# Gated linear attention and a gated expert block: the state product over the whole PE array, with a new order of work

## The chip, the cores and the metric

The kernel runs on one core of a Trainium2 chip. The metric is the device time of one execution in microseconds (us). The engines are TensorE (PE: matrix products; PEld is its weight load), VectorE (DVE), ScalarE (ACT), GpSimd (POOL) and SyncE (SP, which here only starts DMAs).

## The reference

Four batches of eight heads run a decayed linear attention over 768 steps with heads of 48; its output, 3072 tokens of 384, is normalized and goes through a gated expert layer of width 1536.

```python
for t in range(S):
    state = alpha[:, :, t, :, None] * state + np.einsum('bhd,bhe->bhde', k[:, :, t], v[:, :, t])
    y[:, :, t] = np.einsum('bhd,bhde->bhe', q[:, :, t], state)
...
rms = np.sqrt(np.mean(x * x, axis=-1, keepdims=True) + 1e-06)
xn = x / rms * rms_g
g = xn @ w_gate
silu = g * (1.0 / (1.0 + np.exp(-g)))
return (silu * (xn @ w_val) @ w_out)
```

## The kernel before

**Chunks.** The sequence is cut into 24 chunks of 128 tokens, six for each batch; the program takes the first chunks of the four batches, then the second, and so on, so chunk numbers 0 to 3 are first chunks and have no state yet. Within a chunk the eight heads are four pairs. The two heads of a pair lie on partitions 0 to 47 and 64 to 111 of the tiles for k, q and the state.

**Attention of a chunk** (`attention`, L589). DVE makes the running products of the decay by two scans (L616), multiplies k and q with them (L634, L639), and each is split into a high and a low f16 part (`k_lo` L646, `q_lo` L673, `v_lo` L664; the high parts on ACT). PE forms the scores (`scores`, L709; for first chunks in f32, L717), DVE masks them (L722, L736) and splits them (L776). `output` (L780) then adds two things into the PSUM tile `y`: q times the state of the past chunks (L791) and the masked scores times v (L800). Each f16 product is done in three parts, high by high, high by low and low by high (`SPLIT`). First chunks use f32 scores times v instead (L749). For the state, `s_decay` (L691) makes the decayed state `sd`, ACT copies it to f16 (`s_hi`, L695), DVE forms the residue (`s_lo`, L699), and `sums` (L817) makes the next state's addition from the transposed k. Last, ACT squares `y` (L849), DVE multiplies it with the norm's gains (L869), splits it (L876), and a transposing DMA puts it into `xT`.

**The state product before.** L791 uses tiles of 48 rows by 64 columns: for each pair and each of the three parts, the two heads (rows 0 to 47 and 64 to 111) times the two halves of 64 tokens are four products of 48 columns, 12 a pair and 48 a chunk. Head 0 of all pairs is in one PSUM bank of `y`, head 1 in the other; there is one such `y` tile of two banks (`y=1`).

**Weights** (`decode`, L492). The 64-bit weights are turned into f32 by ACT (L519) and three DVE operations (L528, L531, L536), and split into a high part (ACT) and a low part. The low part comes from DVE (L544), or, for the weights named in `LOW_W`, from PE: `bring` (L549) copies the f32 weight into the `y` tile by a product with the identity, `less` (L556) subtracts the high part, ACT reads the result (L562). `i0` to `i11` are the twelve column blocks of the two input matrices, `o0` to `o5` the pairs of blocks of the output matrix.

**Experts.** Seven groups of 4, 2, 2, 4, 4, 4 and 4 chunks (`GROUPS`). For each group and each of 12 column blocks `expert_in` runs 9 products for the gate and 9 for the value (L1002, 512 columns for a group of four chunks, 256 for two), ACT and DVE make the gated product and split it (L1013, L1019, L486, L1032); then `expert_out` sums over the blocks (L1072), DVE drains (L1083) and a DMA stores. Group 0 runs its first five blocks on chunks 0 and 1 first and then on chunks 2 and 3.

**The order.** Nothing is scheduled by hand: `Plan.order` sorts all steps by a model of each engine with the tables at the top (`COST`, `PACE`, `GAP`, `AHEAD`, `STRIDE`, `LATE`, `HOLD`, `BUFS`); each engine then executes its list strictly in that order. At the end `verdict` sums up checks of the data on DVE and PE (L1181, L1209), and all engines branch on the resulting `flag` (L1238, L1239).

Of the kernel before, what the change touches and what calls it, by code (L numbers as in the profile page):

```python
# [50 lines left out]
LOW_W = ['i0', 'i1', 'o1', 'i11', 'i7']  # L51

BUFS = dict(
    att=3, v=2, kh=2, qp=2, k16=2, q16=2, kT=2, v16=4, gd=2, a16=2, ss=2, dk=1, x32=1, x16=2,
    xT=2, raw=2, wu=2, h16=13, sl=2, h32=3, ob=2, at=3, y=1, mm=3,
# [3 lines left out]
    scan=1.16, rec=0.13, kh=0.6, kl=0.6, vl=0.47, ql=0.62, gd=0.12, sd=0.28, sl=0.27, mask=0.59,  # L59
    al=0.59, st=0.27, ss=0.12, x=0.46, xl=0.53, shift=0.57, sign=0.97, rest=0.88, wl=0.87, ob=0.46,  # L60
    dec=0.1, k16=0.62, v16=0.52, q16=0.62, s16=0.26, a16=0.5, sq=0.58, x16=0.53, st0=0.22,
    abs=0.92, wh=0.83, pow=0.65, sc=0.8, sc32=2.3, y=0.78, y0=0.5, y32=1.85, u=0.45, po=1.48,
    neg=0.3, wid=1.6, wneg=0.45, wl2=0.85,
# [9 lines left out]
PACE = [0.939, 1.309, 1.366, 1.325, 1.11, 1.095, 1.217, 1.519]  # L73
GAP = [0, 9.2, -0.3, -0.8, 7.1, 0.3, 11.3, 10.4]
FIRST_DUE = [-19.3, -19.1, -6.2, -12.5]
AHEAD = [0, 6.1, 6.5, 12.3, 23.9, 15.3, 13.6, 8.2]
STRIDE = [0, 4.9, 9.6, 16.8, 26.0, 20.7, 39.7, 9.1]
LATE = dict(
    abs=-14.0, al=-0.2, gd=2.4, h=-10.0, hl=5.8, k16=12.3, kl=1.0, load=6.5, mask=0.9,
    neg=-4.7, ob=-12.5, po=17.9, q16=4.2, ql=1.2, rec=-4.0, rest=0.6, sc=-10.0, scan=2.8,  # L80
    sd=1.5, shift=-3.4, sign=-6.0, sl=3.9, sq=2.0, ss=-4.6, st=-8.0, u=-15.4, v16=14.9,
    vl=-8.0, wh=8.0, wid=3.9, wl=1.9, wneg=-15.1, x=-5.9, x16=12.4, xl=-4.5, y=-3.4,
)
HOLD = dict(
    c10=51.1, c11=64.8, c2=1.0, c5=9.2, c6=12.0, c7=38.1, c8=98.8, i1=19.5, i10=43.3,
    i11=21.3, i4=33.0, i5=48.0, i6=24.5, i9=26.4, o1=68.1, o3=36.2,
# [252 lines left out]
def tile_attn_moe(  # L339
# [160 lines left out]
    def decode(src, dst, name, col):  # L500
# [44 lines left out]

        def bring():
            t["ps"] = buf(ps_y, [P, 2, 512], F32, "y", name)
            for n in range(2):
                nc.tensor.matmul(  # L549
                    t["ps"][:, n, : NW // 2], same, t["uf"][:, n * (NW // 2) : (n + 1) * (NW // 2)],  # L550
                    start=True, stop=False,
                )

        def less():
            for n in range(2):
                nc.tensor.matmul(  # L556
                    t["ps"][:, n, : NW // 2], minus, dst[:, 0, n * (NW // 2) : (n + 1) * (NW // 2)],
                    start=False, stop=True,
                )
# [12 lines left out]
        if name in LOW_W:  # L572
            ps = ("y", name)
            o0 = add("PE", "wid", bring, [o], [wu, ps])
            o = add("ACT", "wh", high, [o], [wu])
            o = add("PE", "wneg", less, [o, o0], [ps])
            return add("ACT", "wl2", residue, [o], [ps])
# [5 lines left out]
    state_ops = {}  # L583

# [3 lines left out]
    def attention(cc, due):  # L588
# [67 lines left out]
        def v_flat():  # L656
            return t["v16"].rearrange("s x j p e -> s x (j p e)")

        def v_hi():
            t["v16"] = tl(ap, [P, 2, 2, NP, D], F16, "v16")  # L660
            split_hi(v_flat()[:, 0], tiles["v", cc], cc, S_V)
# [27 lines left out]
        def s_decay():  # L689
            st, sd, _ = states[b]  # L690
            nc.vector.tensor_tensor(sd, st, t["gd"].to_broadcast([R, NP, D]), op=ALU.mult)  # L691

        def s_hi():
            _, sd, s16 = states[b]
            nc.scalar.copy(s16[:, 0], sd)  # L695

        def s_lo():
            _, sd, s16 = states[b]
            nc.vector.tensor_tensor(s16[:, 1], sd, s16[:, 0], op=ALU.subtract)  # L699
# [43 lines left out]
        def output32(h):  # L743
            if h == 0:
                t["y"] = tl(ps_y, [P, 2, 512], F32, "y")
            v = tiles["v", cc].rearrange("s (j p e) -> s j p e", j=2, p=NP)
            for p in (2 * h, 2 * h + 1):
                for j in range(2):
                    nc.tensor.matmul(  # L749
                        t["y"][:, j, p * D : (p + 1) * D],  # L750
                        tiles["a16", cc][:, j, p, :],
                        v[:, j, p, :],
# [27 lines left out]
        def output(h):  # L780
            if h == 0:
                t["y"] = tl(ps_y, [P, 2, 512], F32, "y")
            yps = t["y"]
            for p in (2 * h, 2 * h + 1):
                cs = slice(p * D, (p + 1) * D)
                for m, (x, y) in enumerate(() if first else SPLIT):
                    for n in range(2):
                        rows = slice(n * HC, (n + 1) * HC)
                        for j in range(2):
                            r = slice(64 * j, 64 * j + D)  # L790
                            nc.tensor.matmul(  # L791
                                yps[rows, j, cs],
                                t["q16"][r, x, p, rows],
                                states[b][2][r, y, p, :],
                                start=m == 0,
                                stop=False,
                            )
                for j in range(2):
                    for m, (x, y) in enumerate(SPLIT):
                        nc.tensor.matmul(  # L800
                            yps[:, j, cs],
                            a_tile()[:, j, x, p, :],
                            t["v16"][:, y, j, p, :],
                            start=first and m == 0,
                            stop=m == 2,
                        )

        def sums():

            t["u"] = [buf(ps_at, [R, NP, D], F32, "at", (cc, 2 + h)) for h in range(2)]  # L810
            for p in range(NP):
                for m, (x, y) in enumerate(SPLIT):
                    for j in range(2):
                        r = slice(64 * j, 64 if j == 0 else R)
                        for h in range(2):
# [4 lines left out]
                                t["v16"][rows, y, j, p, :],  # L820
# [4 lines left out]
        def s_back():  # L825
            if first:
                states[b] = (
                    const.tile([R, NP, D], F32, name=f"st{b}"),
                    const.tile([R, NP, D], F32, name=f"sd{b}"),
                    const.tile([R, 2, NP, D], F16, name=f"s16{b}"),  # L830
                )
                nc.scalar.copy(states[b][0], t["u"][0])
                return
            st, sd, _ = states[b]
# [10 lines left out]
        def like(x):  # L845
            return x.rearrange("p (j c) -> p j c", c=HW)

        def square():
            nc.scalar.activation(  # L849
                like(junk), t["y"][:, :, :HW], AF.Square, accum_out=ssq[:, cc : cc + 1]  # L850
            )
# [15 lines left out]
        def gain():  # L867
            t["x32"] = tl(ap, [P, DM], F32, "x32")
            nc.vector.tensor_tensor(like(t["x32"]), t["y"][:, :, :HW], like(rg), op=ALU.mult)  # L869
# [48 lines left out]
        else:  # L918
# [4 lines left out]
            sh = add("ACT", "s16", s_hi, [sd, before["y"]])  # L923
            sl = add("DVE", "sl", s_lo, [sh], lock=True)
# [7 lines left out]
        else:  # L932
# [12 lines left out]
            ins = [key("a16"), key("v16"), key("y")] + ([] if first else [key("q16")])  # L945
# [304 lines left out]
def layout(inputs):  # L1250
# [25 lines left out]
    vt = v.reshape(B, NP, 2, n, C, D)[:, :, :, :, ::-1].transpose(0, 3, 4, 2, 1, 5)  # L1276
    vt = np.ascontiguousarray(vt).reshape(B * n, C, H * D)

    def rows(x):

        y = np.asarray(x).reshape((NP, 2, D) + x.shape[1:])
        return np.ascontiguousarray(np.moveaxis(y, 1, 0)).reshape(x.shape)
# [4 lines left out]
        "w_gate": rows(inputs["moe_w_gate"]).view(np.int64),  # L1287
        "w_val": rows(inputs["moe_w_val"]).view(np.int64),
        "w_out": np.ascontiguousarray(inputs["moe_w_out"]).view(np.int64),
        "rms_g": rows(inputs["moe_rms_g"]),  # L1290
# [3 lines left out]
                    x.reshape(B, NP, 2, S, D).transpose(0, 2, 1, 4, 3).reshape(B * H, D, S)  # L1294
# [4 lines left out]
        "rms_col": np.ascontiguousarray(rows(inputs["moe_rms_g"]).reshape(-1, C).T),  # L1299
# [18 lines left out]
```

## Time and profile before

| | |
|---|---|
| median of 3 runs | 555.12 us (555.1 to 555.75) |
| span of the profiled execution | 554.4 us |
| mean granted PE clock | 0.992 |
| PE busy | 524.5 us, 5508 products |
| DVE busy | 399.4 us |
| ACT busy | 238.4 us |
| state products (L791) | 960, 22.4 us busy |
| value products (L800) | 480, 25.9 us busy |

The profile is one execution with the time of every instruction on every engine. In the timelines a row gives start, length, engine, line, operation, tiles, shapes and count; lengths of matrix products overlap, since the array takes the next before the last has left it. In rows of groups stand count, total busy time, mean of one in ns, then the idle time before them and what ended it. A row of waits reads: who waited for whom, us in total, times, longest.

### The profile page before, as it was taken

What the parts mean: (1) busy time and instruction counts of PE and PEld (TensorE: products, weight loads), DVE (VectorE), ACT (ScalarE), POOL (GpSimd) and SP (SyncE); (2) the same over time, 40 slices, a digit from 0 to 9 for tenths busy, and PEclk for the clock granted to TensorE, in tenths of its full rate; (3) what the DMA queues carried; (4) which work ended last, traced back from release to release, by engine and by line L of the source; (5) the groups of instructions that cost most, each with busy time, mean ns of one, the idle gap of its engine ahead of it and who ended that gap; (6) DMA issues with size and microseconds to landing.
All of it is one profiled execution on the core that took longest, in us unless ns stands there. A gap on an engine that the chain in (4) does not pass through costs nothing.

```text
span 554.4 us, 13165 instructions
## 1 busy us (share of the span) xinstructions
PE 524.5 (95%) x5508; PEld 315.3 (57%) x5508; DVE 399.4 (72%) x731; ACT 238.4 (43%) x643; POOL 25.1 (5%) x53
## 2 busy tenths in 40 slices
PE   1868999999999999999999999999999999999994
PEld 1746864556886887554556544556544456544452
DVE  6999999999999999987683688999335343233303
ACT  2355866743564565355432254564133421133300
POOL 2101000001001001100000000010000000000000
PEclk9998999999999999999999999999999999999998
DMA  8997546547435523714033234231200000100001
GB/s 210 269 250 194 168 140 214 172 103 181 131 65 140 130 48 96 176 57 91 16 82 76 80 97 92 38 75 34 71 2 2 15 1 30 43 1 0 1 30 35
DMA packets 59444, 50.65 MB, mean 91 GB/s; under 512 B 39440, under 2 KB 54928, under 8 KB 59376
## 3 DMA queue, kind: packets, MB, share of 16 engines
q1 hardware_dynamic: 59376, 49.72, 35.6%
q8 instruction: 45, 0.74, 0.6%
q14 instruction: 23, 0.19, 0.1%
HBM read 35.68 MB, written 4.72 MB: 73 GB/s over the span
## 4 chain that ended last, share of the span: by engine, by line
PE 80%; DVE 13%; issue 3%; DMA 1%; ACT 0%; DVEq 0%; ACTq 0%
PE mm L1002 43%; PE mm_po L1072 24%; PE y L800 4%; PE y L791 3%; PE at L709 3%; DVE dk L616 2%; PE at L817 2%; DVE wu_i L531 1%; DMA kT<-k 1%; DVE h L1019 1%; PE y_i L549 1%; DVE h L1032 1%; DVE wu_i L528 1%; DVE wu_o L531 1%; DVE wu_i L536 1%
## 5 line engine op out<-in xcount | busy, mean ns | idle before, releaser
L1002 PE MATMUL mm<-xT,wg 128*128 128x512 f16 (+1 forms) x1602 | 290.3, 340 | 0.3 <-DVE h L1019 0.3
L1002 PEld LDWEIGHTS <-wg 128*128 128x128 f16 x1602 | 154.5, 98 | 120.5 <-issue 0.7
L1072 PE MATMUL mm_po<-wo,h 128*128 128x384 f16 x864 | 145.8, 326 | 0.0
L1072 PEld LDWEIGHTS <-h 128*128 128x128 f16 x864 | 82.5, 98 | 53.9 <-issue 0.5
L1019 DVE SCALAR_TENSOR_TENSOR h<-mm,sl 128x512 f32<-128x512 f32 (+1 forms) x89 | 51.8, 584 | 51.3 <-PE mm L1002 50.6
L486 ACT ACTIVATE h<-h 128x512 f16<-128x512 f32 (+1 forms) x89 | 48.6, 546 | 83.0 <-DVE h L1019 82.4
L1032 DVE TENSOR_TENSOR h<-h,h 128x512 f16<-128x512 f32 (+1 forms) x89 | 51.8, 583 | 22.2 <-ACT h L486 22.1
L1013 ACT ACTIVATE sl<-mm 128x512 f32<-128x512 f32 (+1 forms) x89 | 45.5, 511 | 40.6 <-PE mm L1002 40.3
L616 DVE TENSOR_TENSOR_SCAN dk<-att,seed 112x520 f32<-112x520 f32 x48 | 59.3, 1236 | 2.8 <-DMA att<-att 2.2
L865 POOL TENSOR_TENSOR ss<-ss,mhalf 128x1 f32<-128x1 f32 x24 | 20.8, 865 | 377.7 <-DVE ss L855 347.1
L1083 DVE TENSOR_SCALAR ob<-mm_po 128x384 f32<-128x384 f32 x24 | 13.2, 551 | 31.3 <-PE mm_po L1072 31.3
L773 ACT CAST a<-at 128x512 f16<-128x512 f32 x40 | 23.1, 584 | 20.0 <-DVE at L722 19.8
L849 ACT ACTIVATE junk<-y 128x384 bf16<-128x384 f32 x24 | 11.7, 489 | 44.8 <-DVE x L869 30.6
L722 DVE TENSOR_TENSOR at<-at,mask 128x512 f32<-128x512 f32 x40 | 26.2, 691 | 0.9 <-PE at L709 0.8
L800 PE MATMUL y<-v,a 128*128 128x48 f16 x480 | 25.9, 185 | 1.0 <-DVE v L664 1.0
L776 DVE TENSOR_TENSOR a<-at,a 128x512 f16<-128x512 f32 x40 | 26.1, 681 | 0.1
L869 DVE TENSOR_TENSOR x<-y,rg 128x384 f32<-128x384 f32 x24 | 13.3, 554 | 17.2 <-PE y L800 14.1
L717 PE MATMUL at<-qp,kh 48*128 48x128 f32 x64 | 8.9, 440 | 14.8 <-DVE qp L639 12.1
L791 PE MATMUL y<-s,q 48*64 48x48 f16 x960 | 22.4, 193 | 0.0
L486 ACT ACTIVATE k<-kh 112x512 f16<-112x512 f32 x24 | 15.0, 626 | 14.5 <-DMA kT<-k 6.0
L791 PEld LDWEIGHTS <-q 48*64 48x64 f16 x960 | 14.1, 106 | 11.1 <-issue 8.6
L800 PEld LDWEIGHTS <-a 128*128 128x128 f16 x480 | 17.3, 96 | 3.8 <-issue 1.1
(104 smaller groups left out, 437.7 us busy)
## 6 DMA issues: line engine op xcount, KB each, us to landing
att<-att SPq DMA_DIRECT2D x22, 675.9 KB, 5.2
v<-vtok SPq DMA_DIRECT2D x24, 192.0 KB, 2.6
raw_i<-w_gate SPq DMA_DIRECT2D x12, 384.0 KB, 3.3
raw_i<-w_val SPq DMA_DIRECT2D x12, 384.0 KB, 4.4
raw_o<-w_out SPq DMA_DIRECT2D x6, 768.0 KB, 4.4
out_dram<-ob SPq DMA_DIRECT2D x24, 192.0 KB, 2.0
att<-att SPq DMA_DIRECT2D x2, 448.0 KB, 7.5
att<-att SPq DMA_DIRECT2D x2, 227.9 KB, 3.0
```

The costliest lines, as they stand in the source:

```text
L486: nc.scalar.activation(dst, src, AF.Copy, scale=scale, accum_out=stat[:rows, col : col + 1])
L616: nc.vector.tensor_tensor_scan(out, x, start.rearrange("r g p c -> r (g p c)"), 0.0, op0=ALU.mult, op1=ALU.add)
L722: nc.vector.tensor_tensor(t["sc"][j], t["sc"][j], mask[:, int(first)].to_broadcast([P, NP, C]), op=ALU.mult,)
L773: nc.scalar.copy(a_tile()[:, j, 0], t["sc"][j])
L776: nc.vector.tensor_tensor(a_tile()[:, j, 1], t["sc"][j], a_tile()[:, j, 0], op=ALU.subtract)
L791: nc.tensor.matmul(yps[rows, j, cs], t["q16"][r, x, p, rows], states[b][2][r, y, p, :], start=m == 0, stop=False,)
L800: nc.tensor.matmul(yps[:, j, cs], a_tile()[:, j, x, p, :], t["v16"][:, y, j, p, :], start=first and m == 0, stop=m == 2,)
L1002: nc.tensor.matmul(ps[:, :n], wg[:, f, x, j, kk, :], xT[:, y, kk, cs], start=i == 0, stop=i == 3 * NK - 1,)
L1013: nc.scalar.activation(t["sl"][:, :n], t[0][:, :n], AF.Silu, scale=1.0 / (S_X * S_W))
L1019: nc.vector.scalar_tensor_tensor(t["h"][:, :n], t[1][:, :n], S_H / (S_X * S_W), t["sl"][:, :n], op0=ALU.mult, op1=ALU.mult,)
L1032: nc.vector.tensor_tensor(h16_of(g, f)[:, 1, cs], t["h"][:, :n], h16_of(g, f)[:, 0, cs], op=ALU.subtract)
L1072: nc.tensor.matmul(t[i][:, :DM], h16_of(g, f)[:, x, ts], wo[:, f // 2, y, f % 2, :], start=f == 0 and m == 0, stop=f == NF - 1 and m == 2,)
```

## The change

**The state product.** The f16 state tile is no longer one per batch but one of two shared ones (`s16=2`), each 112 rows by two parts by four pairs by two heads by 48. For a pair it is a block of 112 by 96: head 0's state stands in rows 0 to 47 and columns 0 to 47, head 1's in rows 64 to 111 and columns 48 to 95, and the rest is zero, set once at the start by POOL. One product over all 112 rows, with q of both heads as weights of 128 columns, then gives both heads for all 128 tokens: three products a pair, 12 a chunk. The heads now lie side by side in `y`, in the order of the reference, so `y` fits one bank, and there are two (`y=2`). The inputs' layout loses its regrouping of heads. `s_hi` and `s_lo` write each head's corner with an operation of its own.

**Weights.** `LOW_W` holds six names in place of five. A weight decoded on PE takes the two `y` banks, and ACT reads each by an operation of its own.

**The order.** All tables of the plan have new values.

```diff
-LOW_W = ['i0', 'i1', 'o1', 'i11', 'i7']
+LOW_W = ["i0", "i1", "i4", "i5", "i6", "o1"]
...
-    xT=2, raw=2, wu=2, h16=13, sl=2, h32=3, ob=2, at=3, y=1, mm=3,
+    xT=2, raw=2, wu=2, h16=13, sl=2, h32=3, ob=2, at=3, y=2, mm=3,
...
-PACE = [0.939, 1.309, 1.366, 1.325, 1.11, 1.095, 1.217, 1.519]
+PACE = [0.871, 1.203, 1.281, 1.428, 1.498, 1.285, 1.581, 1.54]
...
-        def residue():
-            nc.scalar.copy(
-                dst[:, 1].rearrange("p (n c) -> p n c", n=2), t["ps"][:, :, : NW // 2]
-            )
+        def residue(n):
+            nc.scalar.copy(dst[:, 1, half[n]], t["ps"][n][:, : NW // 2])
...
+    s16_tiles = [
+        const.tile([R, 2, NP, 2, D], F16, name=f"s16{n}") for n in range(BUFS["s16"])
+    ]
+    for x in s16_tiles:
+        nc.gpsimd.memset(x, 0.0)
...
-        def s_lo():
-            _, sd, s16 = states[b]
-            nc.vector.tensor_tensor(s16[:, 1], sd, s16[:, 0], op=ALU.subtract)
+        def s_lo(j):
+            sd, s16 = states[b][1], s16_tile()
+            r = slice(64 * j, 64 * j + D)
+            nc.vector.tensor_tensor(s16[r, 1, :, j], sd[r], s16[r, 0, :, j], op=ALU.subtract)
...
-                    for n in range(2):
-                        rows = slice(n * HC, (n + 1) * HC)
-                        for j in range(2):
-                            r = slice(64 * j, 64 * j + D)
-                            nc.tensor.matmul(
-                                yps[rows, j, cs],
-                                t["q16"][r, x, p, rows],
-                                states[b][2][r, y, p, :],
-                                start=m == 0,
-                                stop=False,
-                            )
+                    nc.tensor.matmul(
+                        yps[:, 2 * p * D : 2 * (p + 1) * D],
+                        t["q16"][:, x, p, :],
+                        s16_tile()[:, y, p].rearrange("r j e -> r (j e)"),
+                        start=m == 0,
+                        stop=False,
+                        skip_group_check=True,
+                    )
```

**Two places of the new order.** The first is DVE's list at the start, up to `kh` of chunk 3, the last operand of that chunk's scores. Before (`kh_382` is chunk 3's, `x_1` chunk 1's, `k_1` and `k_2` the k splits of chunks 1 and 2, `wu_i_247` and `wu_i_370` the second and third weight):

```order
L876 SCALAR_TENSOR_TENSOR x_1_362<-x_1_355,ss_278,x_1_362 128x384
L544 TENSOR_TENSOR wg<-wu_i_247,wg 128x768
L841 SCALAR_TENSOR_TENSOR st_349<-at_3_295,st_349 112x192
L646 TENSOR_TENSOR k_1_189<-kh_185,k_1_189 112x512
L646 TENSOR_TENSOR k_2_344<-kh_249,k_2_344 112x512
L528 TENSOR_SCALAR wu_i_370<-wu_i_370 128x768
L531 SCALAR_TENSOR_TENSOR wu_i_370<-raw_i_255,wu_i_370 128x768
L634 TENSOR_TENSOR kh_382<-att_176,dk_284 112x2x4x64
```

And now (`kh_395` is chunk 3's; `wu_i_262` is again the second weight, `a_2` chunk 2's masked scores):

```order
L880 SCALAR_TENSOR_TENSOR x_1_308<-x_1_300,ss_291,x_1_308 128x384
L751 TENSOR_TENSOR a_2_319<-at_0_272,mask 128x512
L751 TENSOR_TENSOR a_2_319<-at_1_273,mask 128x512
L537 SCALAR_TENSOR_TENSOR wu_i_262<-raw_i_167,wu_i_262 128x768
L848 SCALAR_TENSOR_TENSOR st_132<-at_3_326,st_132 112x192
L656 TENSOR_TENSOR k_1_201<-kh_197,k_1_201 112x512
L674 SCALAR_TENSOR_TENSOR v_2_312<-v_248,v_2_312 128x384
L644 TENSOR_TENSOR kh_395<-att_188,dk_294 112x2x4x64
```

The third weight's shift and sign, the second weight's residue and chunk 2's k split have moved behind this `kh`; chunk 2's v split has moved ahead of it. On PE, chunk 2's `y` now stands ahead of chunk 3's scores, and chunk 3's scores are followed by the first expert products.

The second place is DVE's list at the program's end, from the last reduction of the checks to the branch (`at_pok` is PE's last small product, `ob_3` the last drain). Before:

```order
L1206 TENSOR_REDUCE raw_work<-raw_work 128x1
L1211 COPY raw_work<-at_pok 1x1
L1212 TENSOR_SCALAR raw_work<-raw_work 1x1
L1220 CAST flag<-raw_work 1x1
L1083 TENSOR_SCALAR ob_3_7881<-mm_po_3_7823 128x384
L1238 TENSOR_LOAD flag
L1239 COMPARE_AND_BRANCH
```

And now:

```order
L1212 TENSOR_REDUCE raw_work<-raw_work 128x1
L1089 TENSOR_SCALAR ob_3_7214<-mm_po_3_7158 128x384
L1217 COPY raw_work<-at_pok 1x1
L1218 TENSOR_SCALAR raw_work<-raw_work 1x1
L1226 CAST flag<-raw_work 1x1
L1244 TENSOR_LOAD flag
L1245 COMPARE_AND_BRANCH
```

The last drain has moved ahead of the flag. On PE, the small product `at_pok` stood nine expert products before the end and is now the last.

More of the change, by code (lines that the diff above doesn't have):

```diff
@@ L544, in low @@
             nc.vector.tensor_tensor(dst[:, 1], t["uf"], dst[:, 0], op=ALU.subtract)
+        half = [slice(n * (NW // 2), (n + 1) * (NW // 2)) for n in range(2)]
         def bring():
-            t["ps"] = buf(ps_y, [P, 2, 512], F32, "y", name)
+            t["ps"] = [buf(ps_y, [P, 512], F32, "y", (name, n)) for n in range(2)]
             for n in range(2):
                 nc.tensor.matmul(
-                    t["ps"][:, n, : NW // 2], same, t["uf"][:, n * (NW // 2) : (n + 1) * (NW // 2)],
-                    start=True, stop=False,
+                    t["ps"][n][:, : NW // 2], same, t["uf"][:, half[n]], start=True, stop=False
                 )
@@ L572, in decode @@
         if name in LOW_W:
-            ps = ("y", name)
-            o0 = add("PE", "wid", bring, [o], [wu, ps])
+            ps = [("y", (name, n)) for n in range(2)]
+            o0 = add("PE", "wid", bring, [o], [wu] + ps)
             o = add("ACT", "wh", high, [o], [wu])
-            o = add("PE", "wneg", less, [o, o0], [ps])
-            return add("ACT", "wl2", residue, [o], [ps])
+            o = add("PE", "wneg", less, [o, o0], ps)
+            o = add("ACT", "wl2", lambda: residue(0), [o], ps[:1])
+            return add("ACT", "wl2", lambda: residue(1), [o], ps[1:])
         o = add("ACT", "wh", high, [o], [wu])
@@ L583, in tile_attn_moe @@
     state_ops = {}
+    for b in range(NB):
+        states[b] = (
+            const.tile([R, NP, D], F32, name=f"st{b}"),
+            const.tile([R, NP, D], F32, name=f"sd{b}"),
+        )
[4 more added lines that the diff above has]
+        nc.gpsimd.memset(x, 0.0)
     def load_rg():
@@ L922, in attention @@
             sd = add("DVE", "sd", s_decay, [gd, before["st"], before["sl"]], [key("gd")], lock=True)
-            sh = add("ACT", "s16", s_hi, [sd, before["y"]])
-            sl = add("DVE", "sl", s_lo, [sh], lock=True)
+            sh0 = add("ACT", "s16", lambda: s_hi(0), [sd], [key("s16")])
+            sh1 = add("ACT", "s16", lambda: s_hi(1), [sd], [key("s16")])
+            sl = add("DVE", "sl", lambda: s_lo(0), [sh0], [key("s16")], lock=True)
+            sl = add("DVE", "sl", lambda: s_lo(1), [sh1, sl], [key("s16")], lock=True)
             sc = add("PE", "sc", scores, [kl, ql], [key("k16"), key("q16"), at0, at1])
```

98 lines of the change are left out of this document (46 added, 52 removed).

## The prediction

> **What bounds the kernel now.** I read the stretches first (busy time of each engine by stretch), then who TensorE (PE) waited for, then the start and the hand-over to the second token group in order of time, and last the end.
>
> ```profile
> PE 524.5 (95%) x5508; PEld 315.3 (57%) x5508; DVE 399.4 (72%) x731; ACT 238.4 (43%) x643; POOL 25.1 (5%) x53
> ...
> core 0: us, PE busy (x) PEld busy (x) DVE busy (x) ACT busy (x) POOL busy (x), PEclk, DMA share, GB/s
> 0.00:60.00 60.00, 39.07 (x320) 31.81 (x321) 52.65 (x85) 27.59 (x73) 7.84 (x28) 0.97 0.91 227
> 60.00:140.00 80.00, 78.69 (x724) 48.06 (x723) 79.27 (x134) 50.61 (x134) 3.00 (x7) 1.00 0.57 164
> 140.00:240.00 100.00, 100.00 (x1558) 74.44 (x1556) 96.24 (x201) 53.56 (x170) 7.17 (x7) 1.00 0.48 112
> 240.00:310.00 70.00, 70.00 (x747) 37.74 (x746) 47.63 (x86) 27.72 (x71) 1.65 (x3) 1.00 0.28 65
> ```
>
> Three regimes stand here. Up to 60 us VectorE (DVE) is full after the first loads (52.65 of 60) and PE has 21 us of holes. From 60 to 240 us both are full: PE 178.7 of 180, DVE 175.5. After that PE alone is full (70.00 of 70) and DVE has room. So PE's own work counts everywhere after 60 us, and DVE's counts as well until about 240.
>
> ```profile
> PE at L717 <- DVE qp L639: 12.1, 2, 10.0
> PE y_i L549 <- DVE x L869: 3.1, 2, 1.6
> PE at L717 <- DVE kh L634: 2.8, 1, 2.8
> ```
>
> The holes of the start: 12.1 us before the first scores, which the change cannot touch, then waits for DVE's products and for the `y` bank that DVE has not read yet.
>
> **The state product.** The next rows are one stretch of PE's timeline (start, length, operation): a score group, then two pairs of heads, each with 12 products with the state (L791) and 6 with values (L800), and nine expert products.
>
> ```profile
> 153.04 0.84 PE L709 MATMUL at<-q,k 48*128 48x128 f16 x24
> 153.81 0.28 PE L791 MATMUL y<-s,q 48*64 48x48 f16 x12
> 154.02 0.32 PE L800 MATMUL y<-v,a 128*128 128x48 f16 x6
> 154.27 0.28 PE L791 MATMUL y<-s,q 48*64 48x48 f16 x12
> 137.28 15.83 PE mm L1002 x144
> ```
>
> From start to start, 12 state products hold PE for 0.21 us (0.22 in the next pair; I use 0.215) and 6 value products for 0.25, 42 ns each. The lengths overlap, so starts are what to subtract. 20 chunks by 4 pairs by 0.215 is 17.2 us. The change puts 3 products over the whole array, 96 columns, in place of the 12: 240 in all. No row has that form. Below, the value product: the same 128x128 weights, 48 columns, 42 ns. Above, the scores: 128 columns, two of them side by side, 24 in 0.77 us, so 64 ns a pair. An expert product of 256 columns takes 15.83/144 = 110 ns, 0.43 ns a column, so 96 columns stream in 41 ns, no longer than a weight load already costs in the value product. I take 46 ns, near the lower row: 11.0 us, a gain of 6.2. With 64 ns the gain is 1.8, with 42 it is 7.1. PE is full from 60 us on, so this is on the path, except for the first two chunks, which fall before the gate treated next: 216 of the 240 products count, a gain of 5.5 us (1.7 to 6.4).
>
> A rule speaks against this: the Trainium skill, TensorE: Matmul & The Clock Gate, section Back-to-back issue gap, gives some 81 ns for each weight load and 128-column matmul in a stream; by it, as an estimate, 240 would cost about 19 us and the part would lose 2 us. The value rows above disagree with a floor of that size, and no run shown here has 96 columns; it enters as a rival.
>
> **The sixth weight decoded on PE.** One weight more has its low half formed by PE (from `i11`, `i7` to `i4`, `i5`, `i6`).
>
> ```profile
> 105.39 1.45 PE L549 MATMUL y_o<-wu_o,same 128*128 128x384 f32 x4
> 107.00 8.94 PE L1072 MATMUL mm_po<-wo,h 128*128 128x384 f16 x54
> ```
>
> From 105.39 to 107.00 PE is taken: +1.6 us, all of it before the gate. DVE is spared one residue (0.95 us below). ACT reads each result in two pieces; at 43% busy this is hidden, and where `i4` is decoded right before its use it costs about a microsecond.
>
> **The start.** What DVE spends on each kind of operation (count, total, mean ns):
>
> ```profile
> L616 DVE TENSOR_TENSOR_SCAN dk<-att,seed 112x520 f32<-112x520 f32 x48 | 59.3, 1236 | 2.8 <-DMA att<-att 2.2
> L634 DVE TENSOR_TENSOR kh<-att,dk 112x512 f32<-112x512 f32 x24 | 16.5, 686 | 2.1 <-DMA att<-att 1.9
> L646 DVE TENSOR_TENSOR k<-kh,k 112x512 f16<-112x512 f32 x24 | 16.4, 685 | 2.1 <-ACT k L486 2.1
> L664 DVE SCALAR_TENSOR_TENSOR v<-v,v 128x384 f16<-128x384 f32 x24 | 13.2, 550 | 0.0
> L531 DVE SCALAR_TENSOR_TENSOR wu_i<-raw_i,wu_i 128x768 int32<-128x768 int32 x12 | 11.5, 957 | 0.4
> L544 DVE TENSOR_TENSOR wg<-wu_i,wg 128x768 f16<-128x768 f32 x8 | 7.6, 951 | 0.0
> L528 DVE TENSOR_SCALAR wu_i<-wu_i 128x768 int32<-128x768 int32 x12 | 6.6, 553 | 0.3 <-ACT wu_i L519 0.3
> L699 DVE TENSOR_TENSOR s<-sd,s 112x192 f16<-112x192 f32 x20 | 6.9, 346 | 0.4 <-ACT s L695 0.4
> ```
>
> And PE's timeline at the fourth chunk (chunk 3):
>
> ```profile
> 37.77 2.08 PE L717 MATMUL at<-qp,kh 48*128 48x128 f32 x16 [2.77 <-DVE kh L634]
> 39.77 3.65 PE L749 MATMUL y<-v,a 128*128 128x48 f32 x16
> 43.22 4.04 PE L1002 MATMUL mm<-xT,wg 128*128 128x256 f16 x18
> 51.33 2.92 PE L549 MATMUL y_i<-wu_i,same 128*128 128x384 f32 x4 [1.65 <-DVE x L869]
> 55.43 0.83 PE L1002 MATMUL mm<-xT,wg 128*128 128x256 f16 x6
> ```
>
> Ahead of `kh` of chunk 3, for which PE waits until 37.77, the new order of DVE has one k split, one shift, one sign and one residue fewer and one v split more: 0.685 + 0.553 + 0.957 + 0.951 - 0.550 = 2.6 us earlier, 35.2. On PE the `y` of chunk 2 (39.77 to 43.22, 3.45 us) now stands ahead of that score, in what was a hole, since two `y` banks exist. The first expert product can follow the score directly: 35.2 + 2.1 = 37.3 in place of 43.22, a gain of 6. The next gate is `i1`, whose decode on PE needs some 7.5 us of DVE rows after that `kh`: about 42.5 in place of 51.33. I carry 6 to 8 us to the second expert column (55.43), and take off what the new order has left for later there: half of chunk 3's `y` (half of 3.65) and one score group (0.8): 3.5 to 5.5. `i4` and `i5`, decoded between expert products, cost a wait of about 1, and the extra weight 1.6. The start is then worth 1 to 3.5 on PE, plus 0.6 for the first two chunks' state products. DVE's own side of the same span is its last x of group 1:
>
> ```profile
> 133.43 0.59 DVE L876 SCALAR_TENSOR_TENSOR x<-x,ss,x 128x384 f16<-128x384 f32 x1
> 137.21 3.01 PE L1002 MATMUL mm<-xT,wg 128*128 128x256 f16 x26
> ```
>
> It ends 3.2 us before group 1's first expert product, with the transposing DMA between them, so this gate is DVE's too. Ahead of that x the new order has two scans, one `kh`, `qp`, q split and k-side sum, one residue and small pieces fewer, two v splits and two state residues more; by the rows above, DVE gets there about 4.5 us earlier. PE is the later of the two; I take 3.0 us for the gate (bounds 1 and 4.5), at 134.2.
>
> **After the gate.** The state residue is now two operations of 48 partitions in place of one of 112: 20 more, at the 346 ns of L699 if length goes by elements per partition: +7 us of DVE, as much on ACT. Until 240 us DVE has 3.8 us free of 100, later 22 of 70; the order puts only 8 of the extra pieces before group 3's last x and takes a residue away, so I expect it hidden, and set 1.0 us of new waits for PE (0 to 3). POOL's two memsets of the state tiles stand at the program's start, long before their first use.
>
> **The end.** The row of a branch is on PE's sequencer.
>
> ```profile
> 545.50 0.19 PE L1209 MATMUL at_pok<-raw_work 128*1 128x1 f32 x2
> 545.62 1.64 PE L1072 MATMUL mm_po<-wo,h 128*128 128x384 f16 x9
> 546.09 0.14 DVE L1220 CAST flag<-raw_work 1x1 int32<-1x1 f32 x1
> 547.30 0.56 DVE L1083 TENSOR_SCALAR ob<-mm_po 128x384 f32<-128x384 f32 x1 [1.07 <-PE mm_po L1072]
> L1239 PEldq COMPARE_BRANCH  x1: 4182/4182/4182, 546.9 to 546.9; - x1
> ```
>
> The flag is ready at 546.2, 1.0 us before PE's last product ends (547.26); PE's branch on it begins at 546.9, lasts 4.18 us and the program closes 3.3 us after. In the new order the last small product stands behind the nine expert products, and DVE drains `ob` before the flag: some 0.56 and three small operations (0.14 each and the gaps), 1.1 us after PE's end, 2.1 later than now in relation to it. If the whole branch moves, the end grows by 2.1; if a part of it only waited for PE to finish, less. I take 1.7 (1.2 to 2.2).
>
> **The sum**, against the profiled span of 554.4: gate -3.0, state product -5.5, new waits +1.0, end +1.7: -5.8, so 548.6. The median of the timed runs is 555.12, 0.7 above this span, which I carry over: 549.3.
>
> **The rivals.**
>
> ```profile
> L1072 PEld LDWEIGHTS <-h 128*128 128x128 f16 x864 | 82.5, 98 | 53.9 <-issue 0.5
> 295.83 0.62 DVE L876 SCALAR_TENSOR_TENSOR x<-x,ss,x 128x384 f16<-128x384 f32 x1 [0.22 <-ACT x L873]
> 310.47 4.05 PE L1002 MATMUL mm<-xT,wg 128*128 128x512 f16 x18
> ```
>
> Slower: the weight load does not hide. A full load lasts 98 ns; if the four small array tiles hid theirs beside each other and three in a row over the whole array cannot, each product costs 98 ns in place of 72 (0.215/3) for its share of the old: 216 x 0.026 = +5.7 in place of -5.5, and the sum is +5.4: 560.5. It ends slower from about 73 ns a product. Against it: value products with the same load, 42 ns apart. By the 81 ns of the Trainium skill's page named above it would be about 557. Chance 0.07.
>
> DVE becomes the bound before group 4. Its last x ends at 296.45 now, 14.0 us before group 4's first expert product at 310.47. The new order puts some 11 us more of DVE work ahead of that x (14 state residues, 4.8 us; two scans, 2.5; one chunk's other pieces and two drains), while PE arrives 3.0 + 3.1 us earlier (ten chunks of state product). With 3 us off for the earlier start, the x would be 3.7 us late if none of DVE's idle time shrank: 552.0 with the new waits counted in. For it: both engines full until 240. Against it: 26 us of DVE idle between 140 and 310, of which 3.7 suffices. Chance 0.15.
>
> The start gives nothing: the waits move to `i1`, `i4` and the second `y` bank, and group 1 begins at 137.2 as now. Then 552.3. For it: both engines are full from 60 to 140. Chance 0.12.
>
> That the change does not do what it says can be left out: the new order shows 240 products of 96 columns.
>
> **How the numbers follow.** The forecast has 0.66. A measurement of this kernel tells about 0.2%, 1.1 us, from no change. Faster by more: 0.63 of the forecast, 0.11 of the DVE rival, 0.09 of the start rival, 0.83 together; slower: 0.07 and 0.01 of each of the two others, 0.09; the rest, 0.08, is the same. The forecast's own ends are -9.7 (-4.5, -6.4, 0, +1.2) at 545.4, and about 552; the range 545.0 to 554.0 takes in the two middle rivals and leaves out the slower one.
>
> **What would show it.** Right: start to start, three state products in 0.13 to 0.15 us; PE full from about 48 us; group 1's first expert product near 134; the branch of PE starting about 1.7 us behind its last product. Wrong: three products in over 0.22 us; DVE named as releaser of expert products after 140 us for more than 3 us; group 1 still at 137.

## The result, and the profile after

| | before | after |
|---|---|---|
| median of the timed runs | 555.43 us (4 runs, 555.1 to 557.89) | 541.55 us (4 runs, 540.62 to 542.35) |
| ratio, 95% interval | | 0.9746 (0.972 to 0.9771) |
| span of the profiled execution | 554.4 us | 538.9 us |

The changed kernel is 13.9 us faster; 549.3 had been forecast, with 545.0 as the lower end. One run of experiment 9 below, 668.03 us at a granted clock of 0.765, is left out of its median. The profiled span is 15.5 us shorter, and since both traces are there, these 15.5 can be laid out over the program. First the totals and the stretches of the changed kernel, the same stretches as shown of before (the last figures of a stretch are the granted PE clock, the DMA share and GB/s):

```profile
PE 510.8 (95%) x4794; PEld 310.3 (58%) x4794; DVE 406.2 (75%) x750; ACT 244.8 (45%) x670; POOL 25.8 (5%) x55
...
0.00:60.00 60.00, 42.61 (x335) 33.74 (x336) 53.91 (x91) 31.02 (x88) 8.83 (x30) 1.00 0.89 224
60.00:140.00 80.00, 78.12 (x703) 48.51 (x701) 79.07 (x130) 50.52 (x137) 3.69 (x7) 1.00 0.62 173
140.00:240.00 100.00, 99.30 (x1210) 71.54 (x1208) 92.12 (x194) 52.42 (x165) 4.77 (x6) 1.00 0.41 95
240.00:310.00 70.00, 70.00 (x796) 40.15 (x795) 62.31 (x120) 34.51 (x92) 3.96 (x5) 1.00 0.38 91
```

PE is as full as before: its busy time fell by 13.7 us (524.5 to 510.8) of the 15.5, so the time went out of PE's own work and little of it out of its waits. DVE has 7 us more work in all (406.2 against 399.4), but less of it from 140 to 240 us (92.12 against 96.24) and more behind (62.31 against 47.63).

The start, the gate (a group's gate is its first expert product; here group 1's) and the `y` block, from PE's timeline:

```profile
35.25 2.08 PE L732 MATMUL at<-qp,kh 48*128 48x128 f32 x16
37.27 3.01 PE L1008 MATMUL mm<-xT,wg 128*128 128x256 f16 x18
41.37 1.56 PE L552 MATMUL y_i<-wu_i,same 128*128 128x384 f32 x4 [1.09 <-DVE wu_i L537]
...
51.08 1.14 PE L1008 MATMUL mm<-xT,wg 128*128 128x256 f16 x9 [1.23 <-DVE h L1025]
...
133.18 7.04 PE L1008 MATMUL mm<-xT,wg 128*128 128x256 f16 x63
...
153.23 0.29 PE L801 MATMUL y<-s,q 112*128 112x96 f16 x3
153.36 0.31 PE L811 MATMUL y<-v,a 128*128 128x48 f16 x6
153.51 0.29 PE L801 MATMUL y<-s,q 112*128 112x96 f16 x3
```

The first expert product starts at 37.27 (before 43.22), group 1's at 133.18 (before 137.21). In the `y` block three state products hold PE for 0.13 us from start to start, and the six value products behind them for 0.15 us. This pair of heads takes 0.28 us (153.23 to 153.51), where the first pair took 0.46 (153.81 to 154.27).

The end: PE's last expert product drains into `ob`, the flag follows, and PE's branch (a row of that line's list) stands behind it.

```profile
530.62 0.19 PE L1215 MATMUL at_pok<-raw_work 128*1 128x1 f32 x2
530.73 0.56 DVE L1089 TENSOR_SCALAR ob<-mm_po 128x384 f32<-128x384 f32 x1 [1.07 <-PE mm_po L1078]
...
531.55 0.14 DVE L1226 CAST flag<-raw_work 1x1 int32<-1x1 f32 x1
```

```profile
L1245 PEldq COMPARE_BRANCH  x1: 4158/4158/4158, 532.4 to 532.4; - x1
```

From these rows and those of before, the span's 15.5 us make three pieces. To group 1's gate: 137.21 to 133.18, -4.0. From there to the end of PE's last product: 410.05 us (137.21 to 547.26) against 397.6 (133.18 to 530.81), -12.4. From there to the end of the span: 7.1 against 8.1, +1.0. The sum is -15.4, which rounding closes. The middle piece is the surprise.

### The profile page after: what moved, and what is told of

Same layout as the page of the kernel before. It is cut to its first block, busy times and chain, and to the rows that moved or that the text cites. A ratio compares the mean times of both kernels' runs of the same rounds, so it can differ in the third digit from the quotient of the medians.

```text
span 538.9 us, 11773 instructions
## 1 busy us (share of the span) xinstructions
PE 510.8 (95%) x4794; PEld 310.3 (58%) x4794; DVE 406.2 (75%) x750; ACT 244.8 (45%) x670; POOL 25.8 (5%) x55
## 4 chain that ended last, share of the span: by engine, by line
PE 69%; DVE 23%; issue 4%; ACT 1%; DVEq 0%; ACTq 0%
PE mm L1008 41%; PE mm_po L1078 21%; DVE dk L626 3%; PE at L724 2%; DVE h L1038 2%; PE y L811 2%; DVE h L1025 2%; DVE wu_i L532 2%; PE y L801 2%; PE at L829 1%; DVE wu_o L532 1%; DVE wu_i L529 1%; DVE wg L545 1%; DVE x L873 1%; DVE wu_o L537 1%
## 5 line engine op out<-in xcount | busy, mean ns | idle before, releaser
L811 PE MATMUL y<-v,a 128*128 128x48 f16 x480 | 23.5, 184 | 0.0
L801 PE MATMUL y<-s,q 112*128 112x96 f16 x240 | 22.9, 205 | 0.0
L811 PEld LDWEIGHTS <-a 128*128 128x128 f16 x480 | 19.4, 96 | 0.0
L877 ACT ACTIVATE x<-x,ss 128x384 f16<-128x384 f32 x24 | 14.6, 610 | 8.9 <-POOL ss L869 5.6
```

Source lines behind the costliest of these rows:

```text
L801: nc.tensor.matmul(yps[:, 2 * p * D : 2 * (p + 1) * D], t["q16"][:, x, p, :], s16_tile()[:, y, p].rearrange("r j e -> r (j e)"), start=m == 0,
L811: nc.tensor.matmul(yps[:, (2 * p + j) * D : (2 * p + j + 1) * D], a_tile()[:, j, x, p, :], t["v16"][:, y, p, j, :], start=first and m == 0 ...
```

## The experiments

**What the `y` block hides.** The single starts of matrix products in the two traces, in us, at the places whose rows are shown above and in the prediction:

```
before, state    153.810 .813 .817 .820   .863 .866 .869 .873   .894 .898 .901 .904
        value    154.023   .062   .087   .112   .137   .162
        state    154.274 .278 .281 .284 ...
after,  state    153.226   .273   .315
        value    153.356   .385   .410   .435   .460   .486
        state    153.511   .553 ...
```

Before, the twelve state products are issued in 0.094 us. Then nothing starts for 0.12 us; the value products follow each other at 25 ns, and again nothing starts for 0.11 us. After, the step from state to value is 41 ns and the step from value to state is 25 ns, like any other. The second pair has no third gap behind it, since an expert product follows its value products in the same form; but the step from an expert product to the first state product takes 202 ns before and 109 after. So a block of two pairs behind an expert product has four gaps before, and none after. What the two kernels differ in at these steps is above all the tile form, the rows by columns of the array that a product takes (`48*64` in its row): 48x64 against 128x128 before, 112x128 against 128x128 after.

Three theories came from this. **A**: each change of the tile form empties the array, about 0.09 us beyond an ordinary step, and the change of the kernel saved eight such steps a chunk. (The experiments test the price of a change of form. Whether the array empties in that time is not shown: at such a step the load of the next weights starts late too, at 154.018 for the product of 154.023, where in one form it starts a whole product ahead, at 153.316 for 153.356. A load of 96 to 98 ns that does not hide would look the same.) **B**: three products are cheaper than twelve in themselves. **C**: the new order made the gain. The seven kernels of the first two sets, and the four of the third, were each timed beside the kernel before (554.85, 555.64 and 555.27 us in the three).

**1. The kernel before, with the pairs' state products together.** Of each half chunk, both pairs' state products stand first, then both pairs' value products: all twelve small products and the old order stay, and only half the form changes go. (`cs` and `start` are adjusted to it.)

```diff
-            for p in (2 * h, 2 * h + 1):
+            pairs = (2 * h, 2 * h + 1)
+            past = pairs
+            for p in () if first else past:
...
+            for p in pairs:
```

> The kernel before, with the state products of two pairs of heads in a row and then the value products of both, so that PE goes to the 48x64 tile form and back once for two pairs. Theory A (each change of tile form empties the array, about 0.09 us, two a pair): 40 of 80 there-and-backs fall away, 40 x 0.18 = 7.2 us of PE, some nine tenths of it on the path: 6.5 us faster, 0.988 of before, and value products 25 ns apart as now. Theory B (three products in place of twelve are cheaper in themselves): no change. Theory C (the new order of work made the gain): no change.

547.82 us, ratio 0.9867 (0.9837 to 0.9897). PE's timeline:

```profile
153.56 0.38 PE L793 MATMUL y<-s,q 48*64 48x48 f16 x24
153.86 0.47 PE L805 MATMUL y<-v,a 128*128 128x48 f16 x12
154.18 1.14 PE L1008 MATMUL mm<-xT,wg 128*128 128x256 f16 x9
```

Two pairs take 0.62 us in place of 0.84 (153.81 to 154.65), with the same 36 products; the value products among themselves follow at 25 ns, and one gap of 118 ns is left ahead of them. Four changes of 0.09 us a chunk over 20 chunks are 7.2 us; 7.0 were measured. B and C had no change.

**2. The same with all four pairs' state products first.** One way there and one back for each chunk.

```diff
-            past = pairs
+            past = range(NP) if h == 0 else ()
```

> The kernel before, with the state products of all four pairs of a chunk first and the value products after: one there-and-back a chunk in place of four. Theory A: 60 of 80 fall away, 10.8 us of PE, 9.7 on the path: 0.9825 of before, and half as much again as with two pairs in a row. Theories B and C: no change.

545.8 us, ratio 0.9835 (0.9814 to 0.9856).

```profile
168.69 0.56 PE L793 MATMUL y<-s,q 48*64 48x48 f16 x48
169.19 0.77 PE L805 MATMUL y<-v,a 128*128 128x48 f16 x24
169.80 1.62 PE L1078 MATMUL mm_po<-wo,h 128*128 128x384 f16 x9
```

48 state products and 24 value products take 1.11 us, where two blocks of two pairs took 1.68. Six changes a chunk fewer are 10.8 us, of which two chunks' 1.1 fall before group 1's gate, and that gate came 0.7 later in its trace (137.9); 9.1 were measured. So the kernel before gains two thirds of the change's time (9.1 of 13.9) by a reordering of one loop, with no new product at all.

**3. The changed kernel with the columns cut again.** Each state product becomes two of 64 tokens. The order, two `y` banks, zero corners and 112 rows stay; only the form differs from the value products' again.

```diff
+                    for n in range(2):
+                        rows = slice(n * HC, (n + 1) * HC)
...
-                        yps[:, 2 * p * D : 2 * (p + 1) * D],
-                        t["q16"][:, x, p, :],
+                            yps[rows, 2 * p * D : 2 * (p + 1) * D],
+                            t["q16"][:, x, p, rows],
```

> The changed kernel with each state product cut into its two halves of 64 tokens, in the form 128x64, which PE can run beside each other: 6 products a pair in place of 3, and the change of tile form is back twice a pair. Theory A (a change of form costs about 0.09 us): some 80 x 0.18 = 14 us of PE come back, less what two halves beside each other spare: 9 to 14 us slower than the changed kernel, 0.99 to 1.0 of before; value products start some 0.1 us after the last state product. Theory B (cost by number of products): a third of the way from 3 to 12, about 5 us slower than the changed kernel. Theory C: as the changed kernel.

555.92 us, ratio 1.001 (0.9995 to 1.0024): the whole gain is gone, some 14 us.

```profile
153.70 0.32 PE L803 MATMUL y<-s,q 112*64 112x96 f16 x6
153.96 0.32 PE L813 MATMUL y<-v,a 128*128 128x48 f16 x6
154.21 0.32 PE L803 MATMUL y<-s,q 112*64 112x96 f16 x6
```

A pair takes 0.50 us (153.704 to 154.206); between the last state product of 153.817 and the first value product at 153.955 lie 0.14 us again. B had this kernel some 5 us slower than the changed one, C no slower; of the three only A comes near the time that was measured. Which difference of form counts can be read here too: 112 against 128 rows costs nothing after the change, 64 against 128 columns costs two gaps a pair. Rows are not free in general: the scores (48x128) have all columns and still show a gap (see the end).

**4. The old order with the new product.** The kernel before with its own tables and its one `y` tile, and the product, state tiles and cornerwise copies of the change.

```diff
+                    nc.tensor.matmul(
+                        yps[:, 0, :DM].rearrange("s (j p e) -> s p j e", j=2, p=NP)[:, p],
+                        t["q16"][:, x, p, :],
+                        s16_tiles[plan.slot["s16", cc]][:, y, p],
...
```

> The kernel before with its old tables and its one y buffer of two banks, but with the state product over the whole array, two zero-cornered state tiles, and the two-piece state copies and residues: the product without the new order. Theories A and B: 14.5 us less PE work; with nine tenths on the path and some 1 to 4 us given back to DVE, which is full until 240 us and has 20 more operations: 9 to 13 us faster, 0.977 to 0.984. Theory C: within 2 us of before.

547.67 us, ratio 0.9863 (0.9838 to 0.9888): less than expected. The step itself is there (0.30 us a pair), but group 3's first expert product comes at 230.3 us, against 229.5 before; the whole 7 us are won behind it. The stretches say why:

```profile
60.00:140.00 80.00, 77.28 (x644) 46.76 (x642) 79.12 (x134) 50.48 (x134) 3.01 (x7) 1.00 0.55 160
140.00:240.00 100.00, 96.62 (x1309) 73.23 (x1308) 98.45 (x209) 56.96 (x178) 5.55 (x7) 1.00 0.48 113
```

PE waits now (96.62 of 100 us busy), and DVE is full to 98.45 of 100: it looks as if with the old order DVE is the bound up to group 3. The next experiment tests that.

**5. The same without any residue of the state.** The operations of the state's residue go (L699 of the kernel before; the low part of both heads' state stays zero). That is 13.9 us less DVE work than in experiment 4, and also 6.9 less than before the change.

```diff
-            sl = add("DVE", "sl", s_lo, [sh], [key("s16")], lock=True)
+            sl = add("DVE", "sl", lambda: None, [sh], [key("s16")], lock=True)
```

> The old tables and one y buffer with the full-array product, as before, but with no residue of the state at all: DVE has 40 operations of 348 ns, 13.9 us, less than in that kernel and 6.9 us less than before the change. If the gain that this kernel missed up to group 3 was DVE's (98.45 of 100 us busy between 140 and 240): group 3's first expert product comes 4 to 7 us earlier than 230.3, and the time is 541 to 544 us, near the changed kernel's. If the cheap product lacks the new order or the second y buffer for another reason: no change, 546 to 548 us.

541.82 us, ratio 0.9757 (0.9737 to 0.9776): group 3's gate at 224.1, 6.2 us earlier.

```profile
140.00:240.00 100.00, 98.57 (x1341) 73.61 (x1339) 96.43 (x198) 58.08 (x179) 5.92 (x8) 1.00 0.45 112
```

So less DVE work gives the missing time. Only about half of the 6.2 us is DVE's directly: 3.0 arise between the gates of groups 1 and 3. The other 3.2 stand at group 1's gate already (134.9 against 138.1), and there PE's clock has a part, by an estimate as large (see "The gate" below): the full clock comes for good at 45.1 us in this trace and at 54.7 in experiment 4's. Whether the freed DVE time brought the clock forward is open.

**6. The new order with the old product.** The kernel before with the new tables and the six names of `LOW_W`, and one `y` tile.

> The kernel before with the new tables and the six names for weights decoded on PE, but with the old state product and the one y buffer: the order without the product. Theories A and B: 0 to 4 us faster, from the start alone (0.993 to 1.0). Theory C: 10 us or more faster.

565.47 us, ratio 1.0187 (1.0165 to 1.0209): slower, which no theory had. Group 1's gate is at 149.7 us, 12.5 later than before. The longest wait for a weight is new, and the products behind it are slow:

```profile
PE mm_po L1073 <- ACT wo L563: 2.7, 1, 2.7
...
120.42 8.99 PE L1073 MATMUL mm_po<-wo,h 128*128 128x384 f16 x44 [2.71 <-ACT wo L563]
...
60.00:140.00 80.00, 73.58 (x690) 43.98 (x689) 77.13 (x123) 51.03 (x133) 2.79 (x7) 0.97 0.60 161
```

Before the change, 54 such products took 8.94 us; here 44 take 8.99, because from 121.6 to 125.0 us the profile has the granted clock at one half, and they start 320 ns apart in place of 162. It is at one half again from 138.6 to 142.0, and in the start up to 56.7. Of the 12.5 us, PE's waits are 3.1, the sixth weight and one more chunk's scores ahead of the gate 2.4, and the half clock some 6.7, an estimate (half of the 13.3 us that PE is busy longer at that clock than before). Why the order with one `y` tile makes PE wait there was not tested; that `bring` and `y` share this tile is a likely reason. So this kernel doesn't measure the order alone. Experiment 3 comes nearer to that: new order, two banks, and a PE cost a little above the old one (0.50 against 0.46 us a pair, 72 pairs behind the gate, some 3 us) give 555.92 against 555.64, so that order and banks by themselves are worth a few us at most. The second bank without the new order was not measured.

**7. The changed kernel without the residue of the second head's state** (its low part is left at zero; 20 DVE operations fewer).

```diff
-            sl = add("DVE", "sl", lambda: s_lo(1), [sh1, sl], [key("s16")], lock=True)
+            sl = add("DVE", "sl", lambda: None, [sh1, sl], [key("s16")], lock=True)
```

> The changed kernel without the low part of the second head's state (left out; its corner stays zero): 20 DVE operations of 348 ns fewer, 7 us of DVE, with the order otherwise the same. If the two-piece residue is hidden, as the prediction took it: within 1 us of the changed kernel. If DVE is on the path up to 240 us: 2 to 5 us faster than the changed kernel.

538.28 us, ratio 0.9682 (0.966 to 0.9704). Its span is 536.6 us, 2.3 under the changed kernel's. Group 2's gate is where it was (175.0 against 175.1 us), group 3's comes 1.2 us earlier (217.5 against 218.7) and PE ends 1.3 us earlier; the other 1.0 lies behind PE's end. So the added residues do cost PE about a microsecond, between 175 and 219 us. The changed kernel's timeline has two waits there, which this kernel's has not; the products behind them start 523 and 721 ns after the one before, in place of 109:

```profile
185.43 1.14 PE L1008 MATMUL mm<-xT,wg 128*128 128x256 f16 x9 [0.25 <-ACT sl L1019]
...
195.07 5.07 PE L1008 MATMUL mm<-xT,wg 128*128 128x256 f16 x45 [0.45 <-ACT sl L1019]
```

ACT is named, and yet they go when DVE has less to do.

**8. The end.** The changed kernel with its checks' steps 8 us earlier in the plan, so that the flag stands ahead of the last drain again.

```diff
-    v = op("DVE", 0.5, lambda: next(it, None), [v], [work, pok], due=now - 2)
+    v = op("DVE", 0.5, lambda: next(it, None), [v], [work, pok], due=now - 10)
```

(The other four steps move by the same 8.) Its first set:

> The changed kernel with the checks' due times 8 us earlier, so that the last small product stands 36 expert products before the end and the flag is ready before the last drain. If PE's branch of 4.16 us behind the flag sets the end: 1.0 to 2.2 us faster than the changed kernel (span about 537.3), with the branch beginning before PE's last product ends. If the last store sets the end: no change.

539.27 us, ratio 0.9703 (0.968 to 0.9726), span 538.0. It was timed again in one set with the changed kernel itself:

> The changed kernel itself once more, timed beside the kernel before and beside the three kernels that follow, so that differences of half a per cent can be read. All theories: 0.972 to 0.977 of the kernel before, about 541.5 us.

> The changed kernel with the checks' steps 8 us earlier in the plan, timed again beside the changed kernel. If the branch on PE, begun when the flag is there, sets the end: 1.5 to 2 us faster than the changed kernel. If the end is now set by DVE's own branch, which stands behind the last drain whatever the flag does: 0.5 to 1.2 us faster, as its first look (0.9 us of span) had it.

The changed kernel took 541.22 us, ratio 0.9751 (0.973 to 0.9772); with the earlier flag 539.87, ratio 0.9721 (0.97 to 0.9743). The intervals overlap; both pairs of traces agree on about 1 us of span (538.9 and 538.0; 539.1 and 538.1). In the second set's trace, the branch line's list:

```profile
L1245 PEldq COMPARE_BRANCH  x1: 3458/3458/3458, 528.8 to 528.8; - x1
...
L1245 DVEq COMPARE_BRANCH  x1: 72/72/72, 532.0 to 532.0; - x1
...
L1245 PEldq EVENT_SEMAPHORE  x1: 51/51/51, 532.3 to 532.3; - x1
L1245 DVEq EVENT_SEMAPHORE  x1: 21/21/21, 535.2 to 535.2; - x1
```

PE is through its branch at 532.3, but DVE, which branches only behind the last drain, passes on at 535.2. So DVE's event is now the later of the two by 2.9 us, which fits an end that waits for it, and of the 3.6 us by which PE's branch moved, 1 arrives. No run moves DVE's branch alone.

**9. The residue on POOL.** The kernel of experiment 8 with the second head's residue formed by POOL.

```diff
-            sl = add("DVE", "sl", lambda: s_lo(1), [sh1, sl], [key("s16")], lock=True)
+            sl2 = op("POOL", 0.6, lambda: s_lo(1, nc.gpsimd), [sh1], [key("s16")], lock=True, late=LATE["sl"])
+            sl = [sl, sl2]
```

> The kernel with the earlier checks, and with the residue of the second head's state formed by POOL in place of DVE: 20 operations of 348 ns, 7.0 us, leave DVE. If DVE's residues stand on the path (without them the span was 2.3 us shorter), 1 to 3 us faster than the kernel with the earlier checks, 537 to 539 us. If POOL's longer time for the same piece (it is in the chain from the decayed state to the product) comes in their place: no faster, or up to 3 us slower.

539.39 us, ratio 0.9717 (0.9696 to 0.9738), not to be told from 539.87. DVE's busy time falls from 406.1 to 400.3 us; POOL takes on average twice DVE's time for the piece:

```profile
L714 POOL TENSOR_TENSOR s<-sd,s 48x192 f16<-48x192 f32 x20 | 13.7, 688 | 218.8 <-issue 117.0 <-ACT s L709 100.3 <-PE mm L1009 1.5
```

Group 2's gate comes 2.5 us later (178.0 against 175.5) and group 3's 0.6 later (219.7 against 219.1). The plan sorts the steps anew for it, so whether the longer piece or the new sorting spoils the 7 us of freed DVE stays open. The fastest kernels with the whole computation are these two, 1.4 to 1.8 us below the changed kernel; their intervals overlap its own, so that this is a hint and no proof.

## Why the prediction failed, point by point

**The state product: the step that failed.** The text set "12 state products hold PE for 0.21 us" and "6 value products for 0.25, 42 ns each", and then took the value products as given. Both lengths held a gap of about 0.09 us in which nothing started: 0.215 was about 0.12 of products and a gap, 0.25 was 0.16 of products and a gap. Three full-array products take 0.13 us, about as much as twelve small ones in a row: in experiment 1 a set of four starts every 32 ns, behind a first step of 0.05. So the saving that I priced, three products for twelve, is nearly nothing, and all of the gain is gaps: 0.464 - 0.283 = 0.181 us a pair, 80 pairs, 14.5 us, where the text had 6.2 for them; 72 of the pairs lie behind the gate, 13.0 us in place of 5.5. That this term had the right sign was therefore luck. My 46 ns for a product were right (41 to 47). The scores' 64 ns, the upper bracket, held a share of a gap too: pairs of them start 56 ns apart.

The rule that bears on this stands in the Trainium skill, TensorEngine Tiling (Array Packing), section Key Properties: a change of the tiling mode drains the engine. It gives no price. The traces agree in that nothing starts for about 0.09 us more at each change, and experiments 1, 2 and 3 with that price; what happens inside the gap they do not show.

The trace of before had it. An expert product behind a value product, both of the full form, starts 25 ns after it (154.626 to 154.651), while a state product behind a value product starts after 112 ns (154.162 to 154.274). The merged rows of the timeline hide this, since the gap is counted into the length of the row before; the single starts show it. The lower end of the range failed with it: it varied the price of the new product and left the neighbour's price fixed. The signs named for a right prediction could not tell either: three products in 0.13 us, group 1's gate near 134 and the branch 1.6 us behind the last product all came, since none of them looks at the value products. One did not come: PE was not full from 48 us on, but busy for 7.28 of the 10 us from 50 to 60.

**The gate**: -4.0 against -3.0, inside 1 to 4.5. Scores of chunk 3 began at 35.25 (35.2 had been worked out) and the first expert product at 37.27 (37.3). The next decode on PE began at 41.37 ("about 42.5") and the second expert column at 44.93, 10.5 earlier than 55.43; the waits for DVE behind it (1.23 at 51.08) and the work left for later gave 6.5 of that back. But the text overlooked PE's clock. In the start of the kernel before, expert products of 256 columns start 213 ns apart (43.22 to 46.84); from 55.43 on it is 109. After the change the step falls from 213 to 109 at 39 us and stays there. Between 50 and 60 us the kernel before has

```profile
50.00:60.00 10.00, 8.67 (x72) 6.22 (x73) 9.43 (x17) 5.50 (x14) 0.73 (x1) 0.83 0.83 194
```

that is, the half clock once more for 3.4 us, and so the decode at 51.33 took 2.92 us where the one at 41.37 takes 1.56. In all, PE is busy at the half clock for about 5.5 us less than before; at the full clock that work takes half as long, so that some 2.7 us are saved, an estimate. So a part of the 4.0, perhaps more than half, is a thing that the sum did not contain, and its closeness to 3.0 is in part luck. What brings the full clock forward was not tested. Behind the gate both traces have it throughout.

**New waits behind the gate**: +0.6 net (12.4 of the 13.0 arrive), against +1.0. Experiment 7 shows that the second head's residues cost 1.2 before group 3, and that the rest of their 7 us is hidden. The residue's cost per operation was right; its row is

```profile
L714 DVE TENSOR_TENSOR s<-sd,s 48x192 f16<-48x192 f32 x40 | 13.9, 348 | 0.5
```

48 partitions take 348 ns, where 112 took 346.

**The end**: +1.0 against +1.7. The branch of PE lasts 4.16 us again and starts 1.6 us behind PE's last product, as the text had it; but what came behind the branch took 2.3 us (536.6 to 538.9), where before it was 554.4 - 546.9 - 4.2 = 3.3. The text followed PE's branch alone. The events behind the branch, before and after:

```profile
L1239 PEldq EVENT_SEMAPHORE  x1: 51/51/51, 551.1 to 551.1; - x1
L1239 DVEq EVENT_SEMAPHORE  x1: 21/21/21, 551.5 to 551.5; - x1
...
L1245 DVEq EVENT_SEMAPHORE  x1: 21/21/21, 536.2 to 536.2; - x1
L1245 PEldq EVENT_SEMAPHORE  x1: 51/51/51, 536.6 to 536.6; - x1
```

Before, DVE's came last, 2.9 us ahead of the span's end; after, PE's does, 2.3 ahead of it. In experiment 8 DVE's is last again, and the span ends 2.9 us behind it again (535.2 to 538.1). So a later branch of PE need not move the end by as much.

**Around the span**: I carried 0.7 us; the run of the trace after took 540.62 with a span of 538.9, 1.7. The runs of the kernel before in the later sets also have 1.7 to 1.8 there, so this is no effect of the change.

**Two sums** of the text were off, and nothing hangs on them: its own upper ends (-1, -1.7, +3, +2.2) add up to 557.6 and not to "about 552", and its terms of the start give 0.9 to 2.9 where it wrote 1 to 3.5.

**The rivals.** The weight load that does not hide fell: 41 to 47 ns a product, not 73 and more. Nor is it near the 81 ns that the Trainium skill, TensorE: Matmul & The Clock Gate, section Back-to-back issue gap, gives for 128 columns and that the prediction named. DVE as the bound before group 4 did not come with the new order. From the gate to PE's last product the waits of PE are one row, and it does not name DVE (though experiment 7 shows that it goes with DVE's work):

```profile
PE mm L1008 <- ACT sl L1019: 0.7, 2, 0.4
```

It was no idle fear, though: experiment 4 is that rival at group 3, with the old order. So the product's gain and the order's shift of DVE work behind 240 us seem to pay together; no run has the new product and the second bank with the old order. The start did give something, and its rival fell.

## What to carry to other kernels

Price a stretch of matrix products by the single starts, not by merged rows: a gap at each change of tile form sits in the length of the row before and looks like the price of a neighbour. Where small tiles alternate with full-array products, put all products of one form together first (9 us here, for one loop reordered), or give the small product the form of its neighbour, filled up with zeros, if that costs no more time. And when one engine gets cheaper by 14 us, look at once for the other that was 4% from full: the same product with the old order gave little more than half.

## What the runs showed of the hardware

A change between 128x128 and the tile forms 48x64 or 112x64 costs about 0.09 us on PE, each way. In the changed kernel the scores (48x128, so fewer rows alone) and the state sums (64x64) still pay it, as their steps to the expert products show (150.120 to 150.268 and 157.764 to 157.882 us); between 112x128 and 128x128 there is none. Without such a change, full-array products with their weight loads start every 25 ns at 48 columns and every 41 to 47 ns at 96, though each load lasts 96 ns, as the groups of the changed kernel have it (weight loads are the PEld rows): the loads hide.

```profile
L811 PEld LDWEIGHTS <-a 128*128 128x128 f16 x480 | 19.4, 96 | 0.0
...
L801 PEld LDWEIGHTS <-q 112*128 112x128 f16 x240 | 14.9, 96 | 4.0
```

By the profile, POOL took 688 ns on average (545 to 1507) for a residue of 48 by 192 that DVE makes in 348. An engine that is not PE may also hold the end: in experiment 8 DVE's branch of 72 ns began at 532.0, and its next event came at 535.2.

The granted clock of PE can be one half in the middle of a kernel: in experiment 6 it was so for 3.4 us each, from 121.6 and from 138.6 us, a microsecond or so behind waits of 2.7 and 1.5 us, and products of 384 columns then started 320 ns apart in place of 162.
